# Three batches go through experts 0 to 3 and then 4 to 7, with the later experts' weights made among the slots

## The chip, the cores and the metric

The kernel runs on one core of a Trainium2 chip. Its engines work side by side, each through its own queue in order: TensorE (PE) multiplies matrices, VectorE (DVE), ScalarE (ACT) and GpSimd (POOL) do elementwise work, and SyncE (SP) issues most of the transfers (DMA). The metric is the device time of one execution in microseconds (us); lower is better.

## What is computed

An attention with a mask by clusters gives `x`, 3072 tokens in 4 batches of 768. A mixture of 8 experts then goes over every token, weighted by `P`:

```python
def _moe_ref(x, w_gate, w1, w2):
    N, D = x.shape                        # 3072, 512
    ...
    for e in range(E):                    # 8 experts
        h = np.maximum(x @ w1[e], 0.0)    # 512 -> 1024
        ye = h @ w2[e]                    # 1024 -> 512
        out += P[:, e:e + 1] * ye
```

All experts see all tokens, so the order of (batch, expert) pairs is free.

## The kernel before

The first 489 us are the attention. After that every pair of a batch and an expert is two products of matrices, layer 1 (`layer1`, line 1554) and layer 2. Numbers are split into a high and a low part of 16 bits, and a product takes three matmuls (high by high, high by low, low by high).

**Seven products.** Layer 1 multiplies 2x2 blocks with seven products instead of eight (Strassen's method in Winograd's form). It needs sums of the blocks of `w1` (`S1` to `S4`) and differences of the blocks of `x` (`T1` to `T4`). A hidden dimension of 1024 is done in four *halves*, `f2` = 0 to 3, 256 columns each; a half has seven products of six matmuls (line 1543), numbered m = 0 to 6. Between them DVE adds PSUM tiles: `u` behind m = 1 and 3, the blocks `B` behind m = 4, 5, 6 (line 1557). There are two PSUM tiles for it, `pa` and `pb`, so the result of product m must be read before product m+2 writes its tile again.

**First stage** (lines 1618 to 1936): batch 0, experts 0 to 6, 28 halves, `t` = 0 to 27. While a half is multiplied, the weights of the next are split and summed (`make_w`) and also stored in DRAM (`w1d`, `w2d`) for later batches. Layer 2 of the half before (`layer2`, line 1799) stands between its products, with eight products in all: 144 matmuls of 512 columns for an expert. Expert 7 is made piece by piece beside it (`last_first`, `last_second`), at hand-written step offsets (`FIRST_AT`, `SECOND_AT`, kept in `chores`).

**Slots** (line 1938 to the end): `slots` is (batch 0, expert 7) and then batches 1, 2 and 3 with experts 0 to 7, 25 slots. Slot n runs layer 1 of its pair in 28 *steps* of one product; between them stand quarters of layer 2 of the slot before (`layer2b`), which here has seven products as well, 252 matmuls of 256 columns (line 2076). Slot 0 has no layer 2 under it. What else a step holds is set by tables: `plan_slot` puts the differences (`minus`, POOL), the high parts (`high`, ACT) and the low parts (`low`, DVE line 1968, `ho<-B`) at steps, the loads of `w2` (`w2o`) eight steps ahead, the gates, and for batch 1 the sums of `w2` that layer 2 needs (`load_second` to `second_store`: load `r`, four sums on POOL, high on ACT line 1985, low on DVE line 1989, store). Each engine's order is pinned step by step (`plan.keep_order`).

**Totals.** `evict` (line 2042) scales a finished tile by its gate and adds it into `C11`, `C12`, `C21`, `C22` or `X` (which belongs to both C22 and C12 and is joined later). A batch's totals stay in the chip's memory over its eight experts and are then stored to `out`. The next batch's `x` blocks are scanned, scaled, split and stored by `next_x` and fetched by `reload_x` during the last half of the batch before. `spread_powers` sends a small array to DRAM and back to all partitions, to find a scale.

Of the kernel before, what the change touches and what calls it, by code (L numbers as in the profile page):

```python
# [166 lines left out]
def attn_moe_kernel(  # L167
# [1450 lines left out]
    with ExitStack() as ax:
# [73 lines left out]
        chores = {}  # L1692

        def spaced(gen, first, offsets):
            for o in offsets:
                chores.setdefault(first + o, []).append(gen)

        def load_last(m, f2):
            t = lastp.tile([P, 1024], F32, name="lr", bufs=2)
            fs = slice(f2 * 2 * P, (f2 + 1) * 2 * P)  # L1700
            if m == 0:
                nc.sync.dma_start(out=t.rearrange("p (c f) -> p c f", c=NC), in_=w1[E - 1, :, fs].rearrange("(c p) f -> p c f", p=P))
            else:
                nc.sync.dma_start(out=t.rearrange("p (j m) -> p j m", j=2), in_=w2[E - 1, fs, :].rearrange("(j p) m -> p j m", p=P))
            return t

        def last_quads():
            return lastp.tile([P, 6 * HD], F16, name="lq")

        def last_sums():  # L1710
            return lastp.tile([P, 1024], F32, name="ls")

        def last_first(f2):
            raw = load_last(0, f2)
            A = raw.rearrange("p (k c t f) -> p t k c f", k=2, c=KC, t=2)
            d = w1d[N1 + f2].rearrange("p (x a c f) -> p x a c f", x=2, a=7, c=KC)
            yield
            nc.scalar.activation(raw, raw, AF.Copy, scale=s1[:, E - 1 : E])
            yield
            y = last_quads().rearrange("p (x a c f) -> p x a c f", x=2, a=3, c=KC)  # L1720
            S_ = last_sums().rearrange("p (o c f) -> p o c f", o=4, c=KC)
            quads = ((slice(A22, A22 + 1), A[:, 0, 1:2]), (slice(A11, A12 + 1), A[:, 1]))
            for o, a in quads:
                nc.scalar.copy(y[:, 0, o], a)
            sums(S_, A[:, 1, 0], A[:, 1, 1], A[:, 0, 0], A[:, 0, 1], nc.gpsimd)
            yield
            for o, a in quads:
                nc.gpsimd.tensor_tensor(out=y[:, 1, o], in0=a, in1=y[:, 0, o], op=ALU.subtract)
            yield
            nc.sync.dma_start(out=d[:, :, A22 : A12 + 1], in_=y)  # L1730
            yield
            y = raw.bitcast(F16).rearrange("p (x o c f) -> p x o c f", x=2, o=4, c=KC)
            nc.scalar.copy(y[:, 0], S_)
            yield
            for o in (0, 2):
                nc.gpsimd.tensor_tensor(out=y[:, 1, o : o + 2], in0=S_[:, o : o + 2], in1=y[:, 0, o : o + 2], op=ALU.subtract)
# [434 lines left out]
```

## Time and profile before

| what | us |
|---|---|
| median of 3 runs | 2282.61 (2281.35 to 2286.6) |
| profiled execution, its own time | 2285.16 |
| its span, first to last instruction | 2283.2 |
| PE busy in the span | 2257.2 |
| DVE busy | 1655.8 |
| POOL busy | 1163.5 |
| ACT busy | 1132.1 |

A profile is one execution. An engine's busy share is an average over stages, so the rows below are read by stage. Slot 0 starts at 905.42 us, slot 1 at 932.91, and from there on a slot takes 54.81 us: slot 3 starts at 1042.53, slot 9 at 1371.39, slot 21 at 2029.11.

### The profile page before, as it was taken

What the parts mean: (1) busy time and instruction counts of PE and PEld (TensorE: products, weight loads), DVE (VectorE), ACT (ScalarE), POOL (GpSimd) and SP (SyncE); (2) the same over time, 40 slices, a digit from 0 to 9 for tenths busy, and PEclk for the clock granted to TensorE, in tenths of its full rate; (3) what the DMA queues carried; (4) which work ended last, traced back from release to release, by engine and by line L of the source; (5) the groups of instructions that cost most, each with busy time, mean ns of one, the idle gap of its engine ahead of it and who ended that gap; (6) DMA issues with size and microseconds to landing.
All of it is one profiled execution on the core that took longest, in us unless ns stands there. A gap on an engine that the chain in (4) does not pass through costs nothing.

```text
span 2283.2 us, 39973 instructions
## 1 busy us (share of the span) xinstructions
PE 2257.2 (99%) x15655; PEld 1539.5 (67%) x15655; DVE 1655.8 (73%) x2710; ACT 1132.1 (50%) x2085; POOL 1163.5 (51%) x1024
## 2 busy tenths in 40 slices
PE   8999999999999999999999999999999999999998
PEld 5666665655555555677777777777777777777777
DVE  6867676868677885788788866776676666666667
ACT  5666776656766763444444433333343333333333
POOL 6677777835577882566566533233332323222233
PEclk9999999999999999999999999999999999999999
DMA  7556576447667743776666644544444553344433
GB/s 161 132 128 163 136 179 159 126 171 245 237 209 221 240 144 124 284 267 211 218 220 224 217 163 166 181 118 152 153 157 139 192 166 130 130 133 137 144 115 102
DMA packets 231029, 393.39 MB, mean 172 GB/s; under 512 B 73000, under 2 KB 157304, under 8 KB 230328
## 3 DMA queue, kind: packets, MB, share of 16 engines
q1 hardware_dynamic: 230696, 390.80, 55.1%
q8 instruction: 123, 2.02, 0.4%
q14 instruction: 66, 0.54, 0.1%
q10 hardware_dynamic: 144, 0.03, 0.0%
HBM read 281.66 MB, written 80.62 MB: 159 GB/s over the span
## 4 chain that ended last, share of the span: by engine, by line
PE 92%; DVE 3%; ACT 1%; DMA 1%; issue 1%; POOL 1%; SPq 0%; DVEq 0%; ACTq 0%; POOLq 0%
PE h_ps L1543 37%; PE pb L2076 13%; PE pc L2076 8%; PE pa L2076 8%; PE av_ps L1161 5%; PE exp_ps L1106 3%; PE max_ps L990 3%; PE o_ps L1806 3%; PE o_ps L1807 3%; PE o_ps L1808 3%; PE exp_ps L1107 3%; PE misc_ps L1203 1%; PE misc_ps L715 1%; DVE mrt L994 1%; PE misc_ps L835 0%
## 5 line engine op out<-in xcount | busy, mean ns | idle before, releaser
L1543 PEld LDWEIGHTS <-wa 128*128 128x128 f16 x5376 | 525.6, 98 | 295.8 <-issue 4.1
L2076 PEld LDWEIGHTS <-ho 128*128 128x128 f16 x6300 | 616.1, 98 | 145.6 <-DVE ho L1968 2.5
L1543 PE MATMUL h_ps<-xsT,wa 128*128 128x384 f16 x3072 | 581.7, 326 | 1.3 <-DVE u L1557 0.9
L1959 POOL TENSOR_TENSOR B<-B,B 128x768 f32<-128x768 f32 x100 | 206.4, 2066 | 512.8 <-DVE ho L1968 495.1
L1543 PE MATMUL h_ps<-xsB,wa 128*128 128x384 f16 x2304 | 436.8, 326 | 0.1
L1968 DVE TENSOR_TENSOR ho<-B,ho 128x768 f16<-128x768 f32 x300 | 366.3, 1222 | 0.1
L2116 ACT ACTIVATE B<-B 128x384 f32<-128x384 f32 x300 | 156.0, 520 | 394.0 <-DVE B L1557 392.5
L2076 PE MATMUL pb<-w2o,ho 128*128 128x256 f16 x2700 | 342.5, 273 | 0.4 <-DVE ho L1968 0.4
L1557 DVE SCALAR_TENSOR_TENSOR u<-h_ps,m 128x384 f32<-128x384 f32 x256 | 141.5, 553 | 250.0 <-PE h_ps L1543 243.4
L1964 ACT CAST ho<-B 128x768 f16<-128x768 f32 x300 | 239.9, 824 | 12.1 <-POOL B L1959 8.6
L994 DVE TENSOR_REDUCE mrt<-max_ps 128x1 f32<-128x512 f32 (+1 forms) x288 | 190.7, 683 | 69.8 <-PE max_ps L990 68.0
L2076 PE MATMUL pa<-w2o,ho 128*128 128x256 f16 x1800 | 228.4, 273 | 1.2 <-DVE ho L1968 1.2
L2076 PE MATMUL pc<-w2o,ho 128*128 128x256 f16 x1800 | 228.4, 273 | 0.2 <-DVE ho L1968 0.2
L1959 POOL TENSOR_TENSOR B<-B,T 128x768 f32<-128x768 f32 x50 | 98.3, 1966 | 242.0 <-DVE ho L1968 219.8
L1128 POOL TENSOR_TENSOR psum<-psum,pe 128x512 f32<-128x512 f32 x150 | 193.9, 1308 | 31.6 <-ACT pe L1113 29.7
L1113 ACT ACTIVATE pe<-exp_ps 128x512 f32<-128x512 f32 x288 | 168.2, 599 | 59.3 <-PE exp_ps L1107 53.5
L1566 ACT ACTIVATE m<-h_ps 128x384 f32<-128x384 f32 x128 | 62.6, 489 | 202.2 <-PE h_ps L1543 202.1
L2114 ACT ACTIVATE B<-h_ps 128x384 f32<-128x384 f32 x100 | 49.1, 491 | 213.2 <-PE h_ps L1543 213.2
L1557 DVE SCALAR_TENSOR_TENSOR B<-h_ps,u 128x384 f32<-128x384 f32 x200 | 110.3, 552 | 50.1 <-PE h_ps L1543 50.0
L1161 PE MATMUL av_ps<-pe,vn 128*64 128x512 f32 (+1 forms) x768 | 134.4, 492 | 0.0
L1808 PE MATMUL o_ps<-wb,hl 128*128 128x512 f16 x336 | 127.3, 379 | 0.0
L1807 PE MATMUL o_ps<-wb,hh 128*128 128x512 f16 x336 | 127.3, 379 | 0.0
(303 smaller groups left out, 3324.6 us busy)
## 6 DMA issues: line engine op xcount, KB each, us to landing
wa<-w1d SPq DMA_DIRECT2D x102, 896.0 KB
w2o<-w2d SPq DMA_DIRECT2D x175, 512.0 KB
raw<-in_moe_w SPq DMA_DIRECT2D x52, 512.0 KB
w1d<-wa SPq DMA_DIRECT2D x26, 896.0 KB
r<-in_moe_w SPq DMA_DIRECT2D x28, 512.0 KB
...
```

The lines of the kernel that those rows point to most:

```text
L994: nc.vector.tensor_reduce(out=t["mr"][:, i0 : i0 + ni, ni - 1], in_=ps.rearrange("p (x c) -> p x c", x=ni), axis=AX, op=ALU.max)
L1113: nc.scalar.activation(pe, ps.rearrange("p (x c) -> p x c", x=ni), AF.Exp, scale=SCALE)
L1128: (nc.gpsimd if e == POOL else nc.vector).tensor_tensor(out=st[:, o : o + N0], in0=old[o], in1=part, op=ALU.add)
L1161: nc.tensor.matmul(av[o, a:z], vn[:, i, :], heads[t]["pe", c][:, i - i0], start=(i == 0), stop=False, skip_group_check=True)
L1543: nc.tensor.matmul(ps[:, 0:HB], wa[:, w_, a, c, :], x[:, x_, c, :], start=(first and s_ == 0), stop=(s_ == len(steps) - 1), skip_group_che ...
L1557: nc.vector.scalar_tensor_tensor(out=t, in0=ps[:, 0:HB], scalar=KAPPA, in1=x, op0=ALU.mult, op1=ALU.add)
L1807: nc.tensor.matmul(po[i], hh[:, t, ti], wbl[:, t], start=False, stop=False)
L1808: nc.tensor.matmul(po[i], hl[:, t, ti], wbh[:, t], start=False, stop=(last and t == 1))
L1959: nc.gpsimd.tensor_tensor(out=t, in0=d[a], in1=d[c], op=ALU.subtract)
L1964: nc.scalar.copy(t[:, 0], blocks[n, g][o])
L1968: nc.vector.tensor_tensor(out=t[:, 1], in0=blocks[n, g][o], in1=t[:, 0], op=ALU.subtract)
L2076: nc.tensor.matmul(ps[:, q], h[:, h_, f, q * P : (q + 1) * P], w[:, 2 * g + f, w_], start=(first and g == 0 and s_ == 0 and q % 2 == 0), s ...
```

## The change

The first stage now holds experts 0 to 3 of batch 0 alone (`K0 = 4`, 16 halves). Then six *stretches* follow: batch 1 with experts 0 to 3, batch 2 with the same, batch 0 with 4 to 7, batch 1 with 4 to 7, batch 2 with 4 to 7, batch 3 with 0 to 7; 28 slots. So experts 4, 5 and 6 of batch 0 have seven products in layer 2, as expert 7 had.

Between a batch's two stretches its totals lie in DRAM (`parked`), and its `x` blocks are fetched again at every start of a stretch. The weights of experts 4 to 7 are made in pieces: a scan (the largest value, for the scale), `piece_first` for `w1`, `piece_second` for `w2`. Expert 4 is scanned, and three of its eight pieces are made, in the first stage; the other pieces are made in slots 4 to 11, two first and two second matrices a slot, and the scans of experts 5 to 7 lie in slots 3 to 8. The sums of `w2` of experts 0 to 3, which batch 1 needs, are made in slots 0 to 3. The input of batch 2 is prepared from slot 0 on, at seven steps a slot (`INPUTS_AT`), that of batch 3 from slot 8 on at four. The small copies of a weight's scale are issued by ACT, not SP. In the last slot's tail the evictions into `X` go through ACT and a join on POOL, and the last gate is computed ten steps earlier.

```diff
-    N1 = NI - NP2
+    K0 = 4
+    N1 = K0 * NP2
+    STRETCHES = [(b, 0, K0) for b in range(1, B - 1)] + [(b, K0, E) for b in range(B - 1)] + [(B - 1, 0, E)]
+    slots = [(b, e) for b, a, z in STRETCHES for e in range(a, z)]
...
-    def spread_powers(am, n, name, use):
+    def spread_powers(am, n, name, use, by=nc.scalar):
...
+    def piece_second(e, f2, at_, quarters=True):
+        raw = load_piece(e, f2, 1, at_("lr"))
...
+        sums(S_, r2[:, 1, 0:HD], r2[:, 0, 0:HD], r2[:, 1, HD:DO], r2[:, 0, HD:DO], nc.gpsimd)
+        yield
+        if quarters:
...
+            for o, a in quads:
+                nc.scalar.activation(y[:, o, 0], a, AF.Copy, scale=scale)
+            yield
+            for o, a in quads:
+                nc.vector.scalar_tensor_tensor(out=y[:, o, 1], in0=a, scalar=scale, in1=y[:, o, 0], op0=ALU.mult, op1=ALU.subtract)
+            yield
+            nc.sync.dma_start(out=w2d[e][:, A22 : A12 + 1, f2], in_=y)
+            yield
...
+        nc.scalar.activation(y[:, :, 0], S_, AF.Copy, scale=scale)
+        yield
+        nc.vector.scalar_tensor_tensor(out=y[:, :, 1], in0=S_, scalar=scale, in1=y[:, :, 0], op0=ALU.mult, op1=ALU.subtract)
...
+        for name, (r, j) in PARTS.items():
+            nc.sync.dma_start(out=parked[0, name], in_=acc[:, r, 3 * j : 3 * j + 3])
...
-        at(base - 1, gate_slot, n)
+        at(base - (11 if n == NS - 1 else 1), gate_slot, n)
...
+        if n in begins and e:
+            for t, name in ((-18, "C21"), (-9, "C11"), (-4, "C22"), (0, "C12")):
+                at(base + t, resume, n, name)
...
+                        if n in ends and i == 1 and count == 27:
...
+                                for q_ in range(3):
+                                    nc.scalar.activation(
+                                        totals["X"][:, q_], tiles[CHAINS[0]][:, q_], AF.Copy, scale=gates_[:, 3 + q_ : 4 + q_]
+                                    )
+                                for name in ("C22", "C12"):
+                                    join(name)
...
-    INPUTS_AT = (8, 15, 22, 25)
+    INPUTS_AT = {n: (3, 7, 11, 15, 19, 22, 25) if n < K0 else (8, 15, 22, 25) for n in range(NS + 1)}
+    INPUTS = {0: 2, 2 * K0: 3}
+
+    at_ = pieces(piecep, 3, 2, 2, 1)
+    SUMS_AT = ((-1, 5, 8, 9, 10), (0, 9, 12, 13, 14), (11, 14, 16, 17, 18), (15, 18, 20, 21, 22))
+    SUMS_ON = ((-11, -5, 0, 1, 2), (-1, 5, 8, 9, 10), (3, 9, 12, 13, 14), (11, 16, 18, 20, 21))
...
+    FIRST_ON = ((4, 10, 12, 14, 15, 15, 16, 18), (12, 17, 18, 20, 21, 21, 22, 24))
+    SECOND_ON = ((-3, 5, 5, 7, 8, 8, 9, 11), (0, 6, 10, 14, 15, 20, 21, 22))
+    SCANS_ON = ((-4, 1), (2, 8), (9, 13), (17, 24))
```

The numbers of such a table are the steps at which the parts of a piece stand; `SUMS_AT` is for slot 0, in the order load, sums, high, low, store.

DVE's queue in slot 0 before, from its first addition on (`h_ps` is a product's tile, `u` and `B` what the additions make):

```order
L1557 SCALAR_TENSOR_TENSOR u_10606<-h_ps,m_10597 128x384
L1557 SCALAR_TENSOR_TENSOR u_10622<-h_ps,m_10597 128x384
L1557 SCALAR_TENSOR_TENSOR B_10631<-h_ps,u_10622 128x384
L1557 SCALAR_TENSOR_TENSOR B_10639<-h_ps,m_10597 128x384
L1557 SCALAR_TENSOR_TENSOR B_10648<-h_ps,u_10606 128x384
```

Nothing but additions stands there. DVE's queue in slot 0 now, from step 6 on (`am<-xqB` finds the largest value of an input block, `lr<-ls` is the low part of four sums of `w2`):

```order
L1562 SCALAR_TENSOR_TENSOR B_8912<-h_ps,u_8856 128x384
L301 TENSOR_REDUCE am_8874<-xqB_8875 128x1
L1562 SCALAR_TENSOR_TENSOR u_8935<-h_ps,m_8924 128x384
L1703 SCALAR_TENSOR_TENSOR lr<-ls,s_92,lr 128x4x256
L1562 SCALAR_TENSOR_TENSOR u_8957<-h_ps,m_8924 128x384
L1562 SCALAR_TENSOR_TENSOR B_8890<-h_ps,u_8957 128x384
L301 TENSOR_REDUCE am_8874<-xqB_8877 128x1
L1562 SCALAR_TENSOR_TENSOR B_8898<-h_ps,m_8924 128x384
```

Two scans of an input and the first low part of sums of `w2` now stand between the additions of that half.

SP's queue around the start of slots before (`xsB`, `xsT` are reloaded input blocks, `r` is a part of `w2`), from the last load of `wa` that slot 0 needs:

```order
L1500 DMA wa<-w1d_128 128x3584
L1500 DMA wa<-w1d_97 128x3584
L1976 DMA r_10748<-in_moe_w 128x2x512
L1972 DMA w2o<-w2d_6258 128x2048
L1500 DMA wa<-w1d_98 128x3584
L1537 DMA xsB_10790<-xsd1B_6266 128x1536
L1537 DMA xsT_10802<-xsd1T_6267 128x1536
```

The loads of `r` were asked for by slot 0 and are for slot 1. SP's queue now, from the last reload for slot 0 on (`lr` is a part of `w2`, `xqB` an input block as it comes from the attention):

```order
L1542 DMA xsB_8754<-xsd1B_6272 128x1536
L1970 DMA parked0C_6306<-acc 128x768
L1970 DMA parked0C_6307<-acc 128x768
L1970 DMA parked0C_6308<-acc 128x768
L1970 DMA parked0C_6309<-acc 128x768
L1501 DMA wa<-w1d_99 128x3584
L1650 DMA lr<-in_moe_w 128x2x512 x2
L1510 DMA xqB_8875<-xd_83 128x2x384
L1510 DMA xqB_8877<-xd_83 128x2x384
L1510 DMA xqB_8879<-xd_83 128x2x384
L1510 DMA xqB_8881<-xd_83 128x2x384
L1501 DMA wa<-w1d_100 128x3584
```

The totals' stores, two loads of `w2` and four of inputs stand at the head of slot 0, and the third load of `w2` stands behind a store of `lr`.

DVE's queue from step 5 of slot 3 before (`ho` are the low parts for layer 2, `acc` an eviction, `am` a scan of an input, `w2s` a low part of sums):

```order
L1557 SCALAR_TENSOR_TENSOR B_12301<-h_ps,m_12187 128x384
L1968 TENSOR_TENSOR ho<-T_12139,ho 128x768
L1557 SCALAR_TENSOR_TENSOR B_12327<-h_ps,u_12212 128x384
L1968 TENSOR_TENSOR ho<-T_12233,ho 128x768
L2050 SCALAR_TENSOR_TENSOR acc<-pc,gates,acc 128x256 x3
L1557 SCALAR_TENSOR_TENSOR u_12375<-h_ps,m_12353 128x384
L1968 TENSOR_TENSOR ho<-B_11650,ho 128x768
L301 TENSOR_REDUCE am_11731<-xqB_11738 128x1
L1989 SCALAR_TENSOR_TENSOR w2s<-s2w,s_92,w2s 128x4x256
L1557 SCALAR_TENSOR_TENSOR u_12424<-h_ps,m_12353 128x384
```

And now from step 5 of slot 5:

```order
L1562 SCALAR_TENSOR_TENSOR B_11971<-h_ps,m_11841 128x384
L1998 TENSOR_TENSOR ho<-T_11791,ho 128x768
L1562 SCALAR_TENSOR_TENSOR B_12001<-h_ps,u_11870 128x384
L1998 TENSOR_TENSOR ho<-T_11891,ho 128x768
L1696 SCALAR_TENSOR_TENSOR lq<-lr,s_92,lq 128x256 x3
L2059 TENSOR_SCALAR acc<-pc,gates 128x256 x3
L1562 SCALAR_TENSOR_TENSOR u_12055<-h_ps,m_12030 128x384
L1998 TENSOR_TENSOR ho<-B_11264,ho 128x768
L1703 SCALAR_TENSOR_TENSOR lr<-ls,s_92,lr 128x4x256
L1562 SCALAR_TENSOR_TENSOR u_12101<-h_ps,m_12030 128x384
```

Three `lq` (the low parts of quarters of `w2`) stand ahead of the eviction and the next `u`; the scan of an input is not in this slot.

## Rows read from the trace of the kernel before

**Rows 1.** Waits of PE (us in total, times, longest):

```profile
PE pa L2076 <- DVE ho L1968: 1.2, 1, 1.2
...
PE h_ps L1543 <- DVE u L1557: 0.9, 2, 0.8
```

**Rows 2.** Busy us (xcount) of PE, PEld, DVE, ACT, POOL in slots 3, 21:

```profile
1042.53:1097.34 54.81, 54.81 (x423) 41.09 (x420) 47.41 (x67) 24.15 (x38) 36.68 (x27) 1.00 0.62 205
2029.11:2083.92 54.81, 54.81 (x423) 41.09 (x420) 35.99 (x61) 20.00 (x34) 15.74 (x9) 1.00 0.42 135
```

**Rows 3.** The same of line 1543: halves 16 to 27, slots 3 to 23:

```profile
721.36:905.42 184.06, 93.83 (x505) 49.29 (x504) 1.00 0.56 186
1042.53:2193.54 1151.01, 669.44 (x3529) 345.21 (x3529) 1.00 0.50 166
```

**Rows 4.** Timeline (start us, us, instructions xcount) of PE, the start of slots:

```profile
897.65 0.38 PE L1806 MATMUL o_ps<-wb,hh 128*128 128x512 f16 x1
...
905.42 1.14 PE L1543 MATMUL h_ps<-xsB,wa 128*128 128x384 f16 x6
906.39 1.14 PE L1543 MATMUL h_ps<-xsT,wa 128*128 128x384 f16 x6
```

**Rows 5.** Timeline of DVE: the six evictions in the tail:

```profile
2258.03 2.43 DVE L2050 SCALAR_TENSOR_TENSOR acc<-pa,gates,acc 128x256 f32<-128x256 f32 x6
```

**Rows 6.** Busy time of each engine and DMA in a full stretch:

```profile
940.00:945.00 5.00, 5.00 (x42) 3.80 (x40) 4.54 (x8) 2.61 (x5) 4.92 (x3) 1.00 1.03 405
```

**Rows 7.** Instructions of lines (xcount: ns min/median/max); the second from a timeline:

```profile
L1968 DVE TENSOR_TENSOR ho<-B,ho x300: 941/949/2560, 930.5 to 2273.2; 128x768 f16<-128x768 f32 x150
...
665.29 2.69 DVE L1757 SCALAR_TENSOR_TENSOR lq<-lr,s,lq 128x256 f16<-128x256 f32 x3
...
L1557 DVE SCALAR_TENSOR_TENSOR u<-h_ps,m x256: 541/557/559, 493.1 to 2242.0; 128x384 f32<-128x384 f32 x128
...
L1989 DVE SCALAR_TENSOR_TENSOR w2s<-s2w,s,w2s x28: 1270/1278/2842, 937.1 to 1296.7; 128x1024 f16<-128x1024 f32 x28
...
L1985 ACT ACTIVATE w2s<-s2w,s x28: 1132/1138/1150, 935.1 to 1294.7; 128x1024 f16<-128x1024 f32 x28
...
L301 DVE TENSOR_REDUCE am<-xqB x12: 935/944/947, 626.1 to 1499.4; 128x1 f32<-128x768 f32 x12
```

**Rows 8.** Timelines of SP and POOL: a load and its first sum:

```profile
966.76 0.54 SPq L1976 DMA_DIRECT2D r<-in_moe_w  x1
...
972.39 0.73 POOL L332 TENSOR_TENSOR s2w<-r 128x256 f32<-128x256 f32 x1 [6.34 <-DMA r<-in_moe_w]
```

**Rows 9.** Waits of SP, columns as in Rows 1:

```profile
SPq L1485 <- DMA amw<-am: 17.1, 5, 5.0
```

**Rows 10.** Timeline of PE: products in slots 3 and 9:

```profile
1054.28 1.14 PE L1543 MATMUL h_ps<-xsB,wa 128*128 128x384 f16 x6
...
1062.10 1.14 PE L1543 MATMUL h_ps<-xsT,wa 128*128 128x384 f16 x6
...
1390.96 0.81 PE L1543 MATMUL h_ps<-xsT,wa 128*128 128x384 f16 x4
```

**Rows 11.** Timeline of DVE in slot 3:

```profile
1052.92 0.55 DVE L1557 SCALAR_TENSOR_TENSOR B<-h_ps,u 128x384 f32<-128x384 f32 x1
...
1058.39 1.27 DVE L2050 SCALAR_TENSOR_TENSOR acc<-pc,gates,acc 128x256 f32<-128x256 f32 x3 [0.92 <-PE pc L2076]
1059.58 0.55 DVE L1557 SCALAR_TENSOR_TENSOR u<-h_ps,m 128x384 f32<-128x384 f32 x1
```

**Rows 12.** Timeline of DVE in slot 9:

```profile
1385.65 2.44 DVE L2050 SCALAR_TENSOR_TENSOR acc<-pa,gates,acc 128x256 f32<-128x256 f32 x6
...
1389.18 0.55 DVE L1557 SCALAR_TENSOR_TENSOR u<-h_ps,m 128x384 f32<-128x384 f32 x1
```

**Rows 13.** Timeline of DVE: scales of an expert, first and last:

```profile
710.36 0.42 DVE L1489 TENSOR_REDUCE gmax<-all 128x2 f32<-128x256 f32 x1 [1.59 <-DMA all<-amw]
...
711.68 0.55 DVE L1557 SCALAR_TENSOR_TENSOR u<-h_ps,m 128x384 f32<-128x384 f32 x1
```

More of the change, by code (lines that the diff above doesn't have):

```diff
@@ L1612, in attn_moe_kernel @@
     before = iter(())
-    N1 = NI - NP2
+    K0 = 4
+    N1 = K0 * NP2
+    STRETCHES = [(b, 0, K0) for b in range(1, B - 1)] + [(b, K0, E) for b in range(B - 1)] + [(B - 1, 0, E)]
+    slots = [(b, e) for b, a, z in STRETCHES for e in range(a, z)]
+    NS = len(slots)
+    SLOT = 7 * NP2
+    begins, ends, stretch = set(), set(), {}
+    for i, (b, a, z) in enumerate(STRETCHES):
+        begins.add(len(stretch))
+        for _ in range(a, z):
+            stretch[len(stretch)] = i
+        ends.add(len(stretch) - 1)
@@ L1615, in attn_moe_kernel, with stored_at, spaced, load_piece @@
+    def stored_at(q):
+        n, f2 = divmod(q - N1, NP2)
+        return slots[n][1] * NP2 + f2
     PARTS = {"C11": (0, 0), "C22": (1, 1), "C12": (0, 1), "C21": (1, 0)}
     accb = pool("accb", 1)
+    parked = {(b, name): dram.tile([P, 3, HD], F32, name=f"parked{b}{name}") for b in range(B - 1) for name in PARTS}
+    chores = {}
+    def spaced(gen, first, offsets):
+        for o in offsets:
+            chores.setdefault(first + o, []).append(gen)
+    def load_piece(e, f2, m, t):
+        fs = slice(f2 * 2 * P, (f2 + 1) * 2 * P)
+        if m == 0:
+            nc.sync.dma_start(out=t.rearrange("p (c f) -> p c f", c=NC), in_=w1[e, :, fs].rearrange("(c p) f -> p c f", p=P))
+        else:
+            nc.sync.dma_start(out=t.rearrange("p (j m) -> p j m", j=2), in_=w2[e, fs, :].rearrange("(j p) m -> p j m", p=P))
+        return t
@@ L1690, in make_w @@
             yield
[L1692 to L1736, printed above, removed]
-            yield
-            nc.sync.dma_start(out=d[:, :, S1 : S4 + 1], in_=y)
-            yield
@@ L2064, in layer2b @@
             w = lefts.pop((n, i))
[L2065 removed]
+            into = INTO[i][:1] if n in ends and i == 0 else INTO[i]
             for name, j in into:
                 if name not in totals:
[L2068 to L2069 removed]
+                    totals[name] = home(n, name)
             count = 0
@@ L2142, in attn_moe_kernel @@
                 f(*a)
-            if s in INPUTS_AT:
+            for x in chores.pop(now, ()):
+                step(x)
+            if s in INPUTS_AT[n]:
                 step(inputs)
@@ L2146, in attn_moe_kernel @@
             plan.keep_order()
+    assert not tasks and not chores
     assert not tasks
```

230 lines of the change are left out of this document (126 added, 104 removed).

## The prediction

> **What bounds the kernel now.** I read the waits of TensorE (PE) first, then stretches of its products, then the queues beside it in the slots. PE waits for almost nothing: 0.9 us in all for a `u` of VectorE (DVE) and 1.2 us in the tail [rows 1], and in a slot it is busy 54.81 of 54.81 us [rows 2]. So the time is PE's own rows, and a change can only win by fewer of them or lose by making PE wait. DVE and GpSimd (POOL) in turn have room that differs by slot: slot 21 (no weights made) has DVE busy 36.0 us and POOL 15.7; slot 3, in which four sums of a second matrix are made, has 47.4 and 36.7 [rows 2]. The 21 slots from 1042.53 on hold 3528 products' matmuls (the view counts one more at the edge) in 1151.01 us [rows 3], so a slot is 168/3528 of that, 54.81 us: no slot waits.
>
> **The products that go.** Halves 16 to 27 of the first stage and its last, lone layer 2 take 184.06 us [rows 3]; the lone layer 2 runs from 897.65 to 905.42, 7.77 us [rows 4], and after the change half 15 ends in one like it. So 176.29 us go. Three slots of 54.81 us come, 164.43. That is -11.86 us, a sure term: it holds three experts' eighth product (144 matmuls of 512 columns against 252 of 256) and some 1.1 us of small waits that those halves had.
>
> **The tail.** The last gate moves ten steps up, and the six evictions of `X` (2.43 us on DVE [rows 5]) become three on ScalarE (ACT) and two joins on POOL. Behind those evictions stood the `ho` for which PE waited 1.2 us [rows 1]. I take -1.2; the bounds are 0 (the joins hold up the next eviction of C22, which needs them) and -2.4 (all six).
>
> **The first slot after the switch.** Slot 0 has no layer 2 under it, so its steps are 0.97 us [rows 4] and not 1.96. Before, DVE had only the five additions of a half in it. Now its queue also has four `largest` of the next input and four `lr<-ls` (the low half of a sum of w2), and DVE takes them in order: a late load stops PE. Times from the slot's start: the SP queue first has four parked totals (they wait for the last gated eviction, about 1.3), then `wa`, two `lr`, four `xqB`. Ahead of the first `xqB` are 4x384+896+2x512 KB, 3.5 MB, 8.7 us at 405 GB/s, the rate of a full stretch [rows 6], and its own 384 KB are 1.0: it lands at 11.0 and is wanted in step 7, at 6.8. `largest` takes 0.94 [rows 7], the addition behind it 0.55, and the product of step 10, due at 9.75, starts at 12.7: 3.0 lost. The first `lr` lands at about 9.3; four sums of 0.73 on POOL [rows 8], 1.14 on ACT and 1.28 on DVE [rows 7] end at 14.7, the next addition at 15.2, and step 12, by then due at 14.6, starts at 15.4: 0.8. The third `lr` is issued behind the store that waits for this 14.7, at 15.7. Where POOL waited for such a load, it began 5.1 us after the issue's end (967.30 to 972.39 [rows 8]): 20.8, then 2.9, 1.14 and 1.28, and the addition of step 18 ends at 26.7; step 20, due at 23.3, starts at 26.9: 3.6. The fourth goes the same way, 0.6. Sum: **+8.0**. With every landing at 3.4 us and no queue (the mean wait for a copy of 1 KB [rows 9]) the same working gives 3.7; with 7 us it gives about 12.
>
> **Making experts 4 to 7 in slots 4 to 11.** The room is read in slot 3, step by step: `B` of step 4 ends at 1053.47, and the product that needs its tile starts at 1054.28, 0.8 later; `u` of step 8 ends at 1060.13 and its tile is needed at 1062.10, 2.0 later, and DVE was idle for 0.9 just before [rows 10, 11]. A second matrix now puts three `lq` between: 2.69 us together where POOL ran beside them [rows 7], once with 0.8 us of PE waiting for the `u` behind them, the longest wait of its kind [rows 1]. 2.0+0.9 against 2.7 and some longer `ho`: 0.1 a slot, 0.8 over eight. Slots 4 and 8 follow an end of a stretch, with six evictions at step 6; slot 9 of before, which has these, shows `u` ending at 1389.73 and the tile needed at 1390.96, 1.2 of room and no idle time [rows 10, 12]: 2.7 less 1.2 is 1.5 each, 3.0. Slots 5, 7 and 9 have the scales of an expert at step 3, 1.32 us (710.36 to 711.68 [rows 13]), where the room is 0.8: 0.9 each with what is left over at step 8, 2.7. Slots 9 and 11 have a `largest` or a split of an input at step 8: 0.5 and 0.5. Sum **+7.5**. The later `lq`, at step 14, replaces an `S` of 1.28 and finds DVE idle time behind it: nothing, unless DVE comes to it late. Bounds: 2, if a wait of PE in one step frees the next; 14, the rival below.
>
> **The rest, +1.** Scales now go through ACT's queue. SP stood 3.4 us on average between the two small copies [rows 9]; ACT would stand there for that less a step of 2.1, twice in the first stage, off PE's path except for a late `m`: 0.5. Here the Trainium skill ("DMA: Bandwidth & Descriptors", Queues, rings and completion order) says that SP and ACT each own a row of rings and that a DMA engine takes turns between rows packet by packet, so that ACT's copies would not stand behind SP's. By that this half would be 0; no row of this trace shows a small copy on ACT beside a full SP queue. Inputs at seven steps of a slot in slots 0 to 3, not four: 0.5 in slot 2. Parked totals and reloaded inputs (some 18 MB more) have over ten us of lead each and lie beside PE. Bounds of the rest: -1 (the first stage's pieces are fewer) to +4.
>
> **Sum.** -11.9 -1.2 +8.0 +7.5 +1.0 = +3.4 us on the profiled execution's 2285.2, 2288.6. That execution is 2.6 above the median of the runs, 2282.6, which the prediction is for: **2286.0**.
>
> **Rivals.** *The loads come in time* (faster): the first slot costs 4, as with 3.4 us a landing, the making 2, the rest nothing: -11.9-1.2+4+2 = -7.1, 2275.5. For it: slots 1 to 7 of before carry POOL and DVE work for w2 without one wait of PE. Against: there a load stands six or seven steps of 1.96 us ahead of its first use, here three to nine of 0.97. *DVE fills up* (slower): a `low` (`ho<-B`) takes 0.95 in the median and up to 2.56, while an addition that reads PSUM takes 0.54 to 0.56 always [rows 7]; so DVE's steps with two inputs in SBUF wait for POOL. POOL will be busy for most of slots 4 to 11. If the 14 `low` of a slot take 1.75 each, half way, DVE needs 36.0 + 14x0.8 + two times 2.7 for `lq` + two `S` of 2.0, 56.6 us; what is beyond 54.8 is PE's time: 1.8 us in eight slots, 14 for the making, -11.9-1.2+8+14+1 = +9.9, 2292.5. It decides from a mean `low` of 1.6 on. The Trainium skill ("SBUF — State Buffer", Who interferes with whom) states it as a rule: a DVE instruction with two SBUF inputs and a GpSimd instruction that reads SBUF exclude each other for their whole length. The trace agrees (0.95 against 2.56). By that rule alone, with POOL always busy, this rival is what happens. *No fewer products*: excluded, since the order has 576 matmuls of 512 columns where there were 1008.
>
> **How the numbers follow.** Forecast 0.40, loads in time 0.25, DVE full 0.35. A measurement of this kernel tells about 0.2% from no change: 4.6 us, so 2278.0 to 2287.2 is "same". The forecast lies near the upper edge and gives some of its 0.40 to slower; the first rival gives most of its to faster. Faster 0.24, same 0.38, slower 0.38. Range 2274 to 2297: below it little of the first rival is left out, above it the outer part of the second, where the first slot costs 12 too.
>
> **What would show it.** Right: PE waits for DVE in slot 0, with DVE behind it waiting for `xqB` and for ACT's `lr`, and slot 0 some 35 us long, not 27.5; slots 4 to 11 at 55 to 57 us, with PE's waits at steps 6 and 10; slots 12 to 26 at 54.81. Wrong: slot 0 at 28 to 31 us (loads early), slots 4 to 11 all at 57 and over (DVE full), or waits of PE for `wa` or `w2o`, of which I expect none.

## The result: 0.9% slower, and where the time went

The changed kernel takes 2305.32 us (median of 4 runs, 2299.33 to 2308.86) against 2283.92 (4 runs) of the kernel before: 1.0091 times, with a 95% interval of 1.0066 to 1.0116. The prediction was 2286.0 with a range of 2274 to 2297; the time lies above it. The profiled execution took 2304.18 us, span 2302.4. Ratios here and below are of fast runs alone, which leaves out one run of `e11_all3` that took 3266.27 us at a mean granted clock of 0.662.

The span grew by 19.2 us. A stage's length is read from the start of its first matmul of line 1548 (1543 before) to that of the next stage; the terms below are such differences:

| where | forecast | measured |
|---|---|---|
| attention (489.02 to 487.28) | 0 | -1.7 |
| products that went, three slots more | -11.9 | -11.9 |
| stage one, halves 6, 7, 12 | within the rest, +1.0 | +3.8 |
| slot 0 (27.49 to 40.58) | +8.0 | +13.1 |
| slots 1 to 3 | within the rest | +1.4 |
| slots 4 to 11 | +7.5 | +14.6 |
| tail (89.69 to 89.68) | -1.2 | 0.0 |

Slots 12 to 26 take 54.81 us each, as before. In slots 4 to 11 nearly all of the excess lies in three places: slot 5 takes 59.08, slot 7 59.48, slot 9 59.97; slots 4, 6 and 10 take 54.81 and slots 8 and 11 55.0 and 55.1.

PE's waits in the changed kernel, where [rows 1] had 0.9 and 1.2 (us in total, times, longest):

```profile
PE h_ps L1548 <- DVE B L1562: 11.2, 5, 3.3
PE h_ps L1548 <- ACT m L1571: 5.1, 2, 2.8
PE h_ps L1548 <- DVE u L1562: 4.7, 1, 4.7
...
PE h_ps L1548 <- DVE c L1562: 1.3, 1, 1.3
```

That is 22 us of waiting in nine places. In slot 0 the queues of SP and DVE and then PE's products show why (timelines: start, us, instructions; in brackets the idle time before and what ended it):

```profile
728.28 5.20 SPq L1970 DMA_DIRECT2D parked0C<-acc  x4
...
734.57 1.50 SPq L1650 DMA_DIRECT2D lr<-in_moe_w  x2
736.12 2.95 SPq L1510 DMA_DIRECT2D xqB<-xd  x4
```

```profile
744.29 0.95 DVE L301 TENSOR_REDUCE am<-xqB 128x1 f32<-128x768 f32 x1 [5.52 <-DMA xqB<-xd]
745.16 0.55 DVE L1562 SCALAR_TENSOR_TENSOR u<-h_ps,m 128x384 f32<-128x384 f32 x1
```

```profile
745.76 5.87 PE L1548 MATMUL h_ps<-xsT,wa 128*128 128x384 f16 x18 [4.66 <-DVE u L1562]
...
755.36 3.09 PE L1548 MATMUL h_ps<-xsT,wa 128*128 128x384 f16 x18
759.70 2.11 PE L1548 MATMUL h_ps<-xsB,wa 128*128 128x384 f16 x12 [1.25 <-DVE B L1562]
...
765.02 2.04 PE L1548 MATMUL h_ps<-xsB,wa 128*128 128x384 f16 x6 [2.23 <-ACT m L1571]
```

The third wait comes by another way: POOL waits for the fourth load of `w2`, ACT for POOL's sums, and the `m` for which PE waits stands behind them in ACT's queue (POOL, then ACT):

```profile
760.51 0.73 POOL L332 TENSOR_TENSOR ls<-lr 128x256 f32<-128x256 f32 x1 [3.83 <-DMA lr<-in_moe_w]
...
763.44 1.15 ACT L1701 ACTIVATE lr<-ls,s 128x1024 f16<-128x1024 f32 x1 [2.77 <-POOL ls L332]
764.50 0.47 ACT L1571 ACTIVATE m<-h_ps 128x384 f32<-128x384 f32 x1
```

The three waits are 8.1 us together. Behind the first, 18 matmuls take 5.87 us; the same 18 take 3.09 at 755.36. The windows say why (PE busy, granted clock as a share of full speed, DMA share, GB/s):

```profile
736.00:741.00 5.00, 5.00 (x32) 1.00 1.00 354
741.00:746.00 5.00, 0.34 (x2) 0.86 1.08 391
746.00:751.00 5.00, 5.00 (x17) 0.50 0.83 288
751.00:756.00 5.00, 5.00 (x31) 0.96 0.67 226
```

PE's granted clock fell from 2.4 to 1.2 GHz (0.50) behind the wait. Slot 0's excess is 13.1; less the waits it is 5.0, most of it matmuls at the lower level.

Slots 5 and 7 lose theirs at the scale of the next expert (DVE, then PE in slot 5):

```profile
1001.03 0.42 DVE L1490 TENSOR_REDUCE gmax<-all 128x2 f32<-128x256 f32 x1 [1.07 <-DMA all<-amw]
...
1002.81 0.65 DVE L266 TENSOR_SCALAR ginv<-gmax 128x2 f32<-128x2 f32 x1
...
1006.10 0.55 DVE L1562 SCALAR_TENSOR_TENSOR B<-h_ps,u 128x384 f32<-128x384 f32 x1
...
1117.09 0.42 DVE L1490 TENSOR_REDUCE gmax<-all 128x2 f32<-128x256 f32 x1 [3.24 <-DMA all<-amw]
...
1117.95 0.17 DVE L266 TENSOR_SCALAR ginv<-gmax 128x2 f32<-128x2 f32 x1
```

```profile
1006.70 1.39 PE L1548 MATMUL h_ps<-xsB,wa 128*128 128x384 f16 x6 [2.43 <-DVE B L1562]
```

DVE stands until the copy back (`all`) has landed, the small chain and six evictions follow, and only then comes the `B` for which PE waits: 2.43 us in slot 5, 3.20 in slot 7, 3.33 in slot 9 (and 1.14 for a `B` of ACT in slot 7). ACT had issued `all` at 995.23, 1109.16 and 1224.04, so it took 5.8, 7.9 and 7.7 us to land. In slot 5 the chain itself took 2.8 us, since it ran beside POOL's sums: its steps of 0.17 took 0.61 to 0.65.

The tail gained nothing. The joins on POOL held up the eviction of C22, and the `ho` behind it came as late as before (DVE, then PE):

```profile
2279.00 1.27 DVE L2061 SCALAR_TENSOR_TENSOR acc<-pc,gates,acc 128x256 f32<-128x256 f32 x3 [1.71 <-POOL acc L2036]
```

```profile
2281.61 2.58 PE L2089 MATMUL pa<-w2o,ho 128*128 128x256 f16 x22 [1.03 <-DVE ho L1998]
```

Stage one lost 4.7 in halves 6 and 7 (16.26 and 17.60 for 14.60 each), 0.9 of which half 12 gave back. On ACT:

```profile
581.46 0.34 ACTq L1483 DMA_DIRECT2D amw<-am  x1
...
590.68 0.33 ACTq L1486 DMA_DIRECT2D all<-amw  x1
591.06 0.72 ACT L1862 ACTIVATE acc<-acc,gates 128x512 f32<-128x512 f32 x1 [3.45 <-DMA amw<-am]
```

A store of 1 KB was 9.2 us on its way; ACT stood 3.45 us at the copy back, and PE waited 2.8 us for the `m` behind it. That is half 7. In half 6 PE waited 1.3 us for a `c` of DVE, the last of PE's waits shown above.

### The profile page after: what moved, and what is told of

It reads as the page before. It is cut to its first block, busy times and chain, and to the rows that moved or that the text cites. A ratio compares the mean times of both kernels' runs of the same rounds, so it can differ in the third digit from the quotient of the medians.

```text
span 2302.4 us, 40962 instructions
## 1 busy us (share of the span) xinstructions
PE 2254.0 (98%) x15979; PEld 1572.0 (68%) x15979; DVE 1686.2 (73%) x2770; ACT 1158.9 (50%) x2142; POOL 1232.1 (54%) x1056
## 4 chain that ended last, share of the span: by engine, by line
PE 88%; DVE 4%; DMA 4%; POOL 2%; ACT 1%; issue 1%; SPq 0%; DVEq 0%; ACTq 0%; POOLq 0%
PE h_ps L1548 35%; PE pb L2089 13%; PE pc L2089 9%; PE pa L2089 8%; PE av_ps L1161 5%; PE exp_ps L1106 3%; PE max_ps L990 3%; PE exp_ps L1107 3%; PE o_ps L1839 2%; PE o_ps L1837 2%; PE o_ps L1838 2%; DMA all<-amw 1%; DMA amw<-am2z 1%; PE misc_ps L1203 1%; DMA lr<-in_moe_w 1%
## 5 line engine op out<-in xcount | busy, mean ns | idle before, releaser
L2089 PEld LDWEIGHTS <-ho 128*128 128x128 f16 x7056 | 691.0, 98 | 164.2 <-DVE ho L1998 2.4
L1989 POOL TENSOR_TENSOR B<-B,B 128x768 f32<-128x768 f32 x112 | 227.3, 2030 | 487.8 <-DVE ho L1998 467.8
L1548 PE MATMUL h_ps<-xsB,wa 128*128 128x384 f16 x2304 | 439.3, 327 | 16.3 <-DVE B L1562 11.2
L1998 DVE TENSOR_TENSOR ho<-B,ho 128x768 f16<-128x768 f32 x336 | 417.3, 1243 | 0.1
L2089 PE MATMUL pb<-w2o,ho 128*128 128x256 f16 x3024 | 383.7, 273 | 0.4 <-DVE ho L1998 0.4
L2139 ACT ACTIVATE B<-B 128x384 f32<-128x384 f32 x336 | 174.5, 520 | 414.4 <-DVE B L1562 412.9
L1994 ACT CAST ho<-B 128x768 f16<-128x768 f32 x336 | 270.0, 824 | 12.1 <-POOL B L1989 10.3
L2089 PE MATMUL pc<-w2o,ho 128*128 128x256 f16 x2016 | 257.8, 274 | 0.2 <-DVE ho L1998 0.2
L2089 PE MATMUL pa<-w2o,ho 128*128 128x256 f16 x2016 | 255.9, 273 | 1.0 <-DVE ho L1998 1.0
L1107 PE MATMUL exp_ps<-qX,kX 98*128 98x256 f32 (+1 forms) x384 | 126.6, 341 | 0.0
L332 POOL TENSOR_TENSOR ls<-lr 128x256 f32<-128x256 f32 x96 | 93.0, 969 | 60.2 <-DMA lr<-in_moe_w 53.9
```

The lines of the kernel that those rows point to most:

```text
L1107: nc.tensor.matmul(o, t["k2"][0:98, ki], t["qa"][0:98, a:z], start=False, stop=True)
L1548: nc.tensor.matmul(ps[:, 0:HB], wa[:, w_, a, c, :], x[:, x_, c, :], start=(first and s_ == 0), stop=(s_ == len(steps) - 1), skip_group_che ...
L1989: nc.gpsimd.tensor_tensor(out=t, in0=d[a], in1=d[c], op=ALU.subtract)
L1994: nc.scalar.copy(t[:, 0], blocks[n, g][o])
L1998: nc.vector.tensor_tensor(out=t[:, 1], in0=blocks[n, g][o], in1=t[:, 0], op=ALU.subtract)
L2089: nc.tensor.matmul(ps[:, q], h[:, h_, f, q * P : (q + 1) * P], w[:, 2 * g + f, w_], start=(first and g == 0 and s_ == 0 and q % 2 == 0), s ...
```

## Experiments

Theory after reading the two traces: the products are saved as forecast, and the loss is waits for transfers, put at places where an engine that PE needs stands in order behind them, plus the slow clock behind the longer waits. Rivals: DVE is full beside POOL (the prediction's third case); ACT's queue is to blame; the slow matmuls have another cause. The lengths in the table come from the profiled execution of each kernel; "slots 1-3" and "4-11" are the excess over 54.81 each. A profile is one execution: those of `e3_inputs`, `e4_slot0` and `e11_all3` were the shortest of their runs, so their spans lie lower than the ratios would have them.

| kernel | half 6 | half 7 | slot 0 | slots 1-3 | 4-11 | span | ratio to before (95%) |
|---|---|---|---|---|---|---|---|
| changed | 16.26 | 17.60 | 40.58 | 1.4 | 14.6 | 2302.4 | 1.0091 |
| e1_sp | 16.25 | 20.06 | 39.91 | 1.3 | 26.7 | 2314.2 | 1.0146 (1.0128-1.0163) |
| e2_early | 16.26 | 16.86 | 39.65 | 1.4 | 9.3 | 2293.2 | 1.0048 (1.0032-1.0065) |
| e3_inputs | 16.26 | 19.28 | 45.53 | 2.4 | 12.8 | 2305.6 | 1.0134 (1.0114-1.0155) |
| e4_slot0 | 16.27 | 15.71 | 30.59 | 4.1 | 13.4 | 2292.2 | 1.0073 (1.0054-1.0091) |
| e5_all | 14.80 | 15.92 | 27.86 | 6.5 | 3.6 | 2285.2 | 1.0024 (1.0014-1.0033) |
| e7_stage | 14.60 | 18.70 | 39.05 | 1.4 | 16.7 | 2305.9 | one run |
| e8_gap | 16.26 | 16.26 | 39.16 | 1.4 | 4.3 | 2291.6 | one run |
| e9_all2 | 14.59 | 19.64 | 28.42 | 2.8 | 2.4 | 2280.2 | 0.9994 (0.9984-1.0003) |
| e10_stage3 | 16.28 | 15.41 | 29.26 | 2.8 | 3.3 | 2277.6 | one run |
| e11_all3 | 16.26 | 14.60 | 29.37 | 2.8 | 3.0 | 2276.1 | 1.0008 (0.9996-1.0020) |

### The scales' copies back on SP

```diff
-    def spread_powers(am, n, name, use, by=nc.scalar):
+    def spread_powers(am, n, name, use, by=nc.sync):
```

> One part undone: the two small copies of a scale (amw, all) go through SP's queue again, nothing else changes. Queue theory: ACT's standing behind its own small copy made halves 6 and 7 of stage one 1.66 and 3.00 us longer, and the late landing of the copy back (5.8, 7.9 and 7.7 us after its issue on ACT, against 4.7 on SP at 705.62 of the kernel before) makes slots 5, 7 and 9 longer. Then halves 6 and 7 return to 14.60 each (-4.7), slots 5, 7 and 9 each lose some 2 of their 4 to 5 extra us, and the time is about 2305 - 4.7 - 6 = 2294. Place theory: the copy back is issued too near its use whichever queue carries it, so halves 6 and 7 return but slots 5, 7 and 9 stay at 58 to 60: about 2300. If neither holds: 2305.

Measured: slower still, and both theories wrong. Halves 6 and 7 did not return, and slots 5, 7 and 9 took 62.8, 62.4 and 65.6 us. On SP a copy stands behind whatever SP waits for: the copy back was issued 5.9 us after slot 5 began, not 2.9, and DVE waited up to 6.3 us for a landing (waits of DVE from 725 to 1350):

```profile
DVE gmax L1490 <- DMA all<-amw: 15.6, 3, 6.3
```

So ACT's queue is not what makes the copies late; it was the better one of the two here.

### The scans and the store of the maxima earlier

```diff
-    SCANS_ON = ((-4, 1), (2, 8), (9, 13), (17, 24))
+    SCANS_ON = ((-6, -1), (0, 5), (6, 11), (12, 17))
...
-        spaced(piece_scale(e, am), SLOT * (n + 2), (-3, -2, 0, 1, 3, 4))
+        spaced(piece_scale(e, am), SLOT * (n + 2), (-9, -8, -6, -5, 3, 4))
```

> One size changed: the scans and the two copies of an expert's scale stand five to eight steps earlier (copy back at step -5 or -6 of the slot, not 0), its DVE chain stays at step 3, and ACT keeps the copies. Landing theory: DVE's wait for the copy back (1.07, 3.24, 3.36 us) is what makes PE wait in slots 5, 7 and 9; without it slots 7 and 9 fall from 59.5 and 60.0 to about 55, slot 5 from 59.1 to about 57 (its chain beside POOL took 2.8 us, not 1.3): 2305 - 4.5 - 5 - 2 = about 2293.5. Chain theory: the chain of 1.3 us and the six evictions behind it are too much for step 3 anyway (room 0.8): all three slots stay at 56 to 57.5, about 2297. Displacement: the scans moved into other steps make slots 4, 6 and 8 longer than 55, and the sum gains less than 5.

Measured: slots 5, 7 and 9 at 55.4, 57.3 and 55.7. DVE does not wait for a landing any more, and at the scale PE waits 0.47, 0.47 and 0.51 us, though the chain stands in the same step: the landing theory, and against the chain theory. The displacement came too: slot 8 now takes 59.93, because ACT stands at the copy back:

```profile
1197.76 0.33 ACTq L1483 DMA_DIRECT2D amw<-am2z  x1
...
1202.78 0.83 ACT L1994 CAST ho<-B 128x768 f16<-128x768 f32 x1
1207.39 0.33 ACTq L1486 DMA_DIRECT2D all<-amw  x1
1207.76 0.49 ACT L2137 ACTIVATE B<-h_ps 128x384 f32<-128x384 f32 x1 [4.15 <-DMA amw<-am2z]
```

The store took 9.6 us, and PE waited 3.3 for the `B`.

### The same, with ten us between store and copy back

The edit, against the run before:

```diff
-        spaced(piece_scale(e, am), SLOT * (n + 2), (-9, -8, -6, -5, 3, 4))
+        spaced(piece_scale(e, am), SLOT * (n + 2), (-9, -8, -3, -2, 3, 4))
```

> As the run with the earlier scans, but the copy back stands at step -3 of the slot, not -6 or -5, so that ACT reaches it ten us after the store of the maxima was issued. Standing theory: slot 8 was 59.9 there because ACT stood 4.15 us at the copy back, waiting for the store to land (9.6 us after its issue), with the evictions of B and m behind it; now slot 8 is 55.0 again, slots 5, 7 and 9 are 55 to 57.5, and the time is 2294 - 5 = about 2289. Rival: the scans themselves, four steps earlier, delay ACT, and slot 8 stays above 57: 2292 to 2294.

Measured: slot 8 at 54.81, slots 5, 7 and 9 at 56.1, 57.3 and 55.0. So the standing theory holds, and the making of four experts costs 4.3 us in all once both landings have time.

### Slot 0: the next input later, alone

```diff
+    INPUTS_AT[0] = (14, 24)
     INPUTS = {0: 2, 2 * K0: 3}
```

> One part moved: the next input's loads stand in step 14 of slot 0 instead of step 3, its first largest in step 24, the rest in slots 1 to 3. Input theory: DVE's 5.5 us behind xqB cost PE 4.7 us of waiting and the slow clock after it 2.8; slot 0 falls from 40.6 to about 33 (what is left are the two waits for the sums, 1.25 and 2.2, and the clock after the second), 2305 - 7.5 = about 2298. Rival: with xqB gone DVE waits for the first lr and the sums behind it instead, slot 0 stays at 38 to 40 us: 2303 to 2305.

Measured: 45.5 us, worse than the rival. With `xqB` gone DVE waits as long for the first sums, whose load had been hidden behind it, and the four `xqB` loads at step 14 now stand ahead of the fourth `lr`:

```profile
745.98 1.35 DVE L1703 SCALAR_TENSOR_TENSOR lr<-ls,s,lr 128x1024 f16<-128x1024 f32 x1 [5.87 <-ACT lr L1701]
...
768.31 1.35 DVE L1703 SCALAR_TENSOR_TENSOR lr<-ls,s,lr 128x1024 f16<-128x1024 f32 x1 [7.22 <-ACT lr L1701]
```

### Slot 0: the loads of w2 first

On top of the edit of `e3_inputs`:

```diff
-            nc.sync.dma_start(out=parked[0, name], in_=acc[:, r, 3 * j : 3 * j + 3])
...
-    SUMS_AT = ((-1, 5, 8, 9, 10), (0, 9, 12, 13, 14), (11, 14, 16, 17, 18), (15, 18, 20, 21, 22))
+    SUMS_AT = ((0, 7, 10, 11, 12), (0, 10, 14, 15, 16), (1, 14, 17, 18, 19), (2, 18, 20, 21, 22))
...
+        at(3 + i, park_first, name)
```

> As the run before it, and in slot 0 the four pieces of w2 are loaded one after the other at steps 0 to 2 (the fourth into the tile that the scans use), ahead of the parked totals, which are stored at steps 3 to 6. Queue theory (slot 0's loss is a matter of when its loads are issued): no wait of PE above 1 us is left in slot 0, which takes 28 to 29 us: 2305 - 12 = about 2293. Rival: the sums on POOL, ACT and DVE are too much beside products of 0.97 us a step, so that waits of 1 to 2 us stay although everything has landed: slot 0 at 31 to 34, 2296 to 2299.

Measured: slot 0 at 30.6, no wait of PE above 0.9 us there, and the clock at full speed: the queue theory, nearly. But slots 1 and 3 now take 1.7 and 2.4 us over 54.81, so the time fell less than slot 0 did. Slot 3 has 57.20 in `e3_inputs` too, with the inputs' remaining steps in it; slot 1 has 54.81 there, so its excess came with the new order of the loads and sums.

### The clock by itself

```diff
+    for n, k in ((17, 6), (18, 8), (21, 10), (22, 12), (23, 14), (24, 18)):
+        at(SLOT * n + 3, stall, slots[n][0], k)
```

`stall` puts k extra reductions into DVE's queue; nothing else changes.

> The changed kernel with DVE delayed on purpose at step 3 of six quiet slots (17, 18, 21, 22, 23, 24): 6, 8, 10, 12, 14 and 18 extra reductions of 384 columns, by some 0.5 us each. With about 2.6 us of room PE should wait about 0.4, 1.4, 2.4, 3.4, 4.4 and 6.4 us. Clock theory: behind waits of above some 2 to 3 us PE's granted clock falls to the lower level for a few us, as behind the waits in slots 0, 5 and 9, so that a slot's excess over 54.81 is the wait and 1.5 to 3 more. Rival: the excess is the wait alone, within 0.3, and the slow matmuls in slots 0, 5 and 9 have another cause.

Measured (room was smaller than expected, so all waits are longer):

| slot | PE waited | excess of the slot | difference |
|---|---|---|---|
| 17 | 1.96 | 2.12 | 0.16 |
| 18 | 3.13 | 3.29 | 0.16 |
| 21 | 4.31 | 6.13 | 1.82 |
| 22 | 5.49 | 6.97 | 1.48 |
| 23 | 6.66 | 9.08 | 2.42 |
| 24 | 9.01 | 10.75 | 1.74 |

The windows after the wait of 3.13 (first two) and of 4.31 (last three), columns as above:

```profile
1740.00:1742.00 2.00, 1.21 (x9) 1.00 0.00 0
1742.00:1744.00 2.00, 2.00 (x18) 1.00 0.55 147
```

```profile
1909.00:1911.00 2.00, 1.31 (x5) 0.67 0.00 0
1911.00:1913.00 2.00, 2.00 (x10) 0.50 0.28 39
1913.00:1915.00 2.00, 2.00 (x17) 0.97 0.83 326
```

The clock theory holds: behind the four longer waits the clock fell and a slot lost 1.5 to 2.4 us beyond its wait; behind the two shorter it did not. In the changed kernel a wait of 2.43 (slot 5) was followed by the lower level and one of 3.20 (slot 7) was not, and in e4 one of 3.13 (slot 7) was, as long as the one here that was not. So the length of the wait does not settle it alone; what does stays open.

### Stage one

Only the start of the next input moved (half 5 for half 3, and one more of its steps in the later halves):

```diff
-            if t == 3:
+            if t == 5:
                 inputs = next_x(1, True)
```

> One part moved: in stage one the next input begins in half 5, not 3 (with one more step in the later halves so that it ends in time); the scales' copies stay on ACT. Collision theory: halves 6 and 7 are long because the input's reductions, subtractions and its own pair of small copies fall into the same halves as the scale of an expert, so that the scale's first copy landed only after 9.2 us; then halves 6 and 7 are 14.6 to 15 each, and no later half is above 15.5: about -4, 2301. Rival: the new order of the scale itself (ACT's queue, one step later) does it, and halves 6 and 7 stay at 16 and 17: 2305.

Measured: half 6 is 14.60, but half 7 is 18.7 and half 9 19.2; the sum is no better, so half of the collision theory stands: the input's work makes half 6 long. In half 7 the scale's store took 8.5 us, and ACT stood 2.7 us at its copy back. In half 9 ACT stood at a copy back again, but for another reason: the 1 KB store had landed 4.9 us after its issue, and the profile puts ACT's wait to a store of `wb` that landed 7.2 us later:

```profile
619.11 0.33 ACTq L1486 DMA_DIRECT2D all<-amw  x1
619.48 0.52 ACT L1913 ACTIVATE hh<-c 128x384 f16<-128x384 f32 x1 [7.12 <-DMA w2d<-wb]
```

The next run puts the copies on ACT in the kernel before, where nothing else was added to these halves:

```diff
-    def spread_powers(am, n, name, use):
+    def spread_powers(am, n, name, use, by=nc.scalar):
...
-        nc.sync.dma_start(out=d, in_=am)
+        by.dma_start(out=d, in_=am)
...
-        nc.sync.dma_start(out=t, in_=d.partition_broadcast(P))
+        by.dma_start(out=t, in_=d.partition_broadcast(P))
```

> One part of the change alone, on the kernel before: the small copies of the experts' scales go through ACT's queue, all else as before. Queue theory: ACT stands at the copy back until the store has landed, with the evictions behind it, so that halves 6 and 7 (14.60 each in the kernel before) grow by 1.5 us or more: 2285 to 2288. Traffic theory: the store lands after 5.4 us as it did on SP, because the loads and stores that the change put into halves 3 to 10 are not there; ACT stands 1 to 2 us with no wait of PE, all halves keep their lengths within 0.3 us, and the time is that of the kernel before, 2283.

Measured: halves 6 and 7 at 14.60 and 14.90, ACT stood 1.0 us (waits of ACT from 480 to 800), and the copy back was issued 5.2 us after the store, where SP of the kernel before needed 5.4:

```profile
ACT acc L1831 <- DMA amw<-am: 1.0, 1, 1.0
```

So the queue alone does not lengthen these halves. That the work put beside it does is shown for half 6 (`e7_stage`) and for half 7 left by elimination only: the DMA engines' busy share from 580 to 590 us is 0.54 in the changed kernel and 0.49 in the one before, so fuller DMA engines do not explain the late store. The median is 2285.8 against 2282.0, 1.0014 (1.0003 to 1.0025): 3 us that neither theory expected, of which the trace shows 1.7 in the first stage, 1.1 of it in half 20.

### All causes removed

Inputs in half 5, e4's loads with DVE's operations in its idle steps of slot 0, e8's scales, and the joins of the tail behind the evictions; its tables:

```diff
+                            if n == NS - 1 and i in (1, 2):
+                                join(("C22", "C12")[i - 1])
...
+    INPUTS_AT.update({0: (8, 23, 27), 1: (3, 6, 9, 12, 15, 18, 21, 25), 2: (3, 6, 9, 12, 15, 18, 21, 25)})
...
+    SUMS_AT = ((0, 3, 7, 8, 9), (0, 7, 12, 13, 14), (1, 11, 14, 15, 16), (2, 15, 19, 20, 21))
```

> All causes found so far removed together: the next input of stage one begins in half 5 and not 3; in slot 0 the four pieces of w2 are loaded at steps 0 to 2 ahead of the parked totals, their DVE operations stand in the steps where DVE was idle (8, 13, 15, 20), and the next input's loads stand in step 8; the scans of experts 5 to 7 and the store of their maxima stand earlier, the copy back at step -3 of the slot, ten steps of time for the two landings; the two joins of the tail come behind the evictions that they held up. If these are the causes, against the changed kernel: stage one -4, slot 0 -11 to -13, slots 5, 7 and 9 -12, tail -1: 2305 - 29 = about 2276, 0.3% under the kernel before. If a moved step only moves its wait (as the scans did to slot 8), some 5 to 8 us of it come back in slots 1 to 3 and 4 to 10: 2282 to 2284, no different from the kernel before.

Measured: slot 0 at 27.9, slots 4 to 11 down to 3.6 of excess, but 6.5 us came back in slots 1 to 3 and 4.4 in halves 7 and 9: the second case. Then a second try (loads of the input before slot 0, one join later, inputs from half 2):

```diff
-            if t == 3:
+            if t == 2:
...
+                    if m == 6:
+                        second = next_x(2)
+                        step(second)
...
-            at(base - SLOT + 14, join, "C12")
+            at(base - SLOT + (14 if n == NS - 1 else 20), join, "C12")
...
+    INPUTS_AT.update({0: (1, 6, 13, 27), 1: (3, 6, 9, 12, 15, 18, 21, 25), 2: (3, 6, 9, 12, 15, 18, 21, 25)})
...
+    SUMS_AT = ((0, 2, 7, 8, 9), (0, 6, 14, 15, 16), (1, 11, 19, 20, 21), (2, 16, 21, 22, 23))
```

> All causes removed together a second time, with what the first try left: in slot 0 the next input's loads are issued before the slot, its reductions and the sums' DVE operations stand in the steps where DVE had been idle, so that it needs no step in slot 3 (55.8 to 57.8 in slots 1 and 3 of the first try came with its splits and late sums); one of the two joins on POOL stands at step 20 of slots 3 and 7, not 14 (ACT waited 5.4 us for POOL's quarters there, PE 1.7); the next input of stage one begins in half 2, so that its pair of small copies is past before the scale's. If these are the causes: stage one +1 over the kernel before, slot 0 at 28, slots 1 to 11 together at most +3 over 54.81 each: span about 2274, time 2275 to 2277, 0.3% under the kernel before. If the waits only move once more: 2282 to 2286.

> The same but for stage one, which is as in the changed kernel (the next input begins in half 3). Collision theory: halves 6 and 7 are 16.3 and 16 to 18 again, some 3 to 5 us more than with half 2, everything from slot 0 on the same. Rival: stage one costs the same in both, wherever the next input begins, because the small copies take 9 us and more beside that stage's full queue whatever lies beside them.

Measured: from slot 0 to slot 11 all that remains is 6.1 us (0.9 + 2.8 + 2.4). Stage one costs 5.2 more than before, so of the 11.9 us saved 11.2 are lost again, and the kernel ties with the one before, 0.9994 (0.9984 to 1.0003), between the two expectations. The largest wait left is the one of half 7 (PE's waits):

```profile
PE h_ps L1548 <- ACT m L1571: 3.8, 2, 3.2
```

With half 3 (e10) halves 6 and 7 cost 16.3 and 15.4, so in these two traces a loss stays in stage one wherever the input begins. In e10 ACT did not stand for the store, which landed within 5.8 us; DVE stood 2.5 us at the copy back of half 7. The last run is e10 with seven stores moved from halves 4 to 10 to halves 8 to 14:

```diff
-            chores.setdefault(7 * (4 + i) + 4, []).append(store_x(0, o))
+            chores.setdefault(7 * (8 + i) + 4, []).append(store_x(0, o))
```

> As e10 (stage one's next input in half 3), and the stores of batch 0's input for its later use stand in halves 8 to 14 of stage one, not 4 to 10. Traffic theory: the scale's 1 KB store took 9 to 12 us to land in halves 6 and 7 because of the stores and loads that the change put there; with seven stores of 384 KB out of the way it lands in 5 to 6 us, as in the kernel before, and halves 6 and 7 take 14.6 to 15.5 each: span about 2275, time 2276 to 2278, under the kernel before by 0.2 to 0.3%. Rival: the landing is as late as before and differs from run to run (half 7 took 15.4 to 21.7 us in the runs so far), so the time stays at 2279 to 2282, no different from the kernel before.

Measured: the profiled execution has half 7 at 14.60 and a span of 2276.1, as the traffic theory said, yet its other runs went up to 2291 (that of 3266.27 aside) and the median is 2284.2, 1.0008 (0.9996 to 1.0020): no gain. A trace shows only one execution, so where the longer ones lose is not shown. Half 7, with the same code in stage one, took 15.4 to 21.7 us in seven traces (the changed kernel's and six of the runs); in the trace of the kernel before it is 14.60.

## Why the prediction was wrong, step by step

- **The products, -11.9.** Right: slots 12 to 26 are 54.81 us, and no wait came with seven products.
- **The first slot, +8.0.** Right in mechanism (waits first for `xqB`, then for the sums' landings), wrong in the sum. That the waits come to 8.1 us is luck in part: step 10 waited 4.7 where 3.0 was put, step 12 not at all (0.8), step 20 1.25 (3.6), and the fourth load cost 2.2 (0.6), by ACT's `m` and not by DVE. The step that failed is a missing term: 5.0 us that follow the waits, with PE at the lower clock level (0.50 from 746 to 751). e6 shows that such a term belongs to a wait: 1.5 to 2.4 us each behind four of six. The two loads hide each other (e3), so the waits cannot be added up or removed one by one, only together (e4).
- **Making experts 4 to 7, +7.5.** Wrong in its parts. The second matrices, priced 0.1 to 1.5 a slot, cost nothing (slots 4, 6, 10). The scales, priced 0.9 each, cost 4.3 to 5.2. The step that failed is "1.32 us (710.36 to 711.68)": it took the busy time of the chain and left out the wait of 1.59 us for the landing that stands in brackets in the same row [rows 13]. In a slot that wait (1.07, 3.24 and 3.36 us in slots 5, 7 and 9) stops DVE, its evictions and PE. e2 and e8 removed it, and at the scale 0.0 to 1.2 us of waiting were left.
- **DVE fills up** (the rival at 2292.5). Its time was the nearest, but it is not what happened: the mean `ho<-B` is 1.32 us (94 from 941 to 1384), under the 1.6 from which it decides, and DVE is busy 45.3 of 54.81 us in slot 4, with PE never waiting (columns as in [rows 2]):

```profile
937.55:992.36 54.81, 54.81 (x423) 41.10 (x421) 45.30 (x73) 34.18 (x58) 41.69 (x33) 1.00 0.89 312
992.36:1051.44 59.08, 56.65 (x423) 41.86 (x421) 46.54 (x77) 34.25 (x58) 40.98 (x33) 0.97 0.86 283
```

- **The rest, +1.0.** Wrong: 5.1. "ACT would stand there for that less a step, twice, off PE's path except for a late `m`: 0.5" is the step. ACT stood once, for 3.45 us, because the store took 9.2 us to land, and PE waited for just that `m`. The forecast's 3.4 [rows 9] is how long SP stood, not a landing: in the kernel before, the same 1 KB stores of the first stage lie 3.0 to 5.4 us ahead of their copies back. The other part is half 6, which the forecast held to be free, and 1.4 in slots 1 to 3, where 0.5 was put. The Trainium skill ("DMA: Bandwidth & Descriptors", Queues, rings and completion order), from which the forecast concluded that ACT's copies would not stand behind SP's, gave 0 here; the conclusion is the forecast's own. The traces bear out neither a quick landing nor a slow queue: 5.2 us on ACT and 5.4 on SP in the same kernel (e12), 9.2 on ACT in the changed one.
- **The tail, -1.2.** Wrong; the lower bound that the text named (the joins hold up the next eviction of C22) is what happened. That the joins alone cost the gain is not shown: with the joins behind that eviction the wait of 1.03 is gone, but two of 0.34 and 0.35 come (e9), and the tail takes 89.5 (e9 to e11) or 90.2 (e5), where it took 89.3 to 90.1 in the runs that left it as it was.
- **Loads come in time.** Wrong: slot 0 took 40.6.

The spans differ by 19.2 us where 3.4 were forecast. Of the 15.8 between, 5.1 are slot 0 (its clock), 7.1 the making, 4.1 stage one and slots 1 to 3, 1.2 the tail; the attention gave back 1.7, which no edit explains (its end lies between 484.9 and 489.4 us in the traces). In the 7.1, slots 5, 7 and 9 cost 14.1 (waits of PE 10.1, and about 1.8 each behind the waits of slots 5 and 9, where the clock fell to 0.50 for some 3 us) where 2.7 were put for the scales; the rest of the making cost 0.5 where 4.8 were put.
